# Router logits of an attention and mixture-of-experts kernel: per tile with the tokens stationary, or per batch of four tiles with the experts stationary

## The chip, the core and the metric

The kernel runs on one core of a Trainium2 chip. A time is the device time of one execution in microseconds. The profile is one execution recorded by the hardware profiler: PE is TensorE's matmuls, PEld its weight loads, DVE VectorE, ACT ScalarE, POOL GpSimd, SP the SyncE queue. "L689" is line 689 of the kernel file.

## The reference

Chunked attention over 8 batches, 8 heads, 576 positions and 64 dimensions (chunks of 64), then a router over 8 experts and the chosen expert's two-layer network for each of the 4608 tokens. All data is float32.

```
scores = q_c @ k_c^T / sqrt(64)              # per chunk of 64
attn   = softmax(scores);  out = attn @ v_c
x      = out as (4608 tokens, 512)
xn, en = x / |x|,  expert_emb / |expert_emb|
logits = xn @ en^T / tau                     # (4608, 8)
expert = argmax(logits)
gate   = softmax(logits)[expert]
y      = gate * (relu(x @ w1[expert]) @ w2[expert])    # 512 -> 1024 -> 512
```

## The kernel before

**Tiles and stages.** The 4608 tokens are 36 tiles (NT) of 128 tokens. A first stage runs attention and routing for tile after tile and writes each token's row, with its eight logits, to a place in DRAM (`spots`) that belongs to its expert. A second stage reads groups of 64 rows of one expert each, two experts at a time, and multiplies them by w1 and w2. The second stage isn't edited.

**The order of the first stage** is written out by hand (a manual schedule: each engine runs its instructions in program order). The loop at L1011 goes over t from -3 to NT + 2 and works on several tiles at once. In iteration t PE does, in this order: `turn_a(t)` (four transposes of the attention weights, L634), `turn_qk(t + 3)` (four transposes of k and four of q, L592), `logits(t - 2)` (L689), `scores(t + 2)` (32 records, L608), every fourth time `place` (L725 to L740), `turn_x(t - 1)` (four transposes of the attention output, L677) and `values(t)` (L648). A float32 matmul leaves two records in the trace, a transpose one.

**Who evicts.** ACT copies aT (L636), kxT (L595) and xT (L679) out of PSUM, squares the row (L682) and takes the exponential (L628). DVE copies qxT (L597), takes the maximum of the scores and subtracts it (L616, L618), divides the output (L656 to L659, tile `xr`), and copies the logits of four tiles (L702). The transposes share three PSUM buffers (`tr`); scores and values have one each (`sc`, `pv`).

**The router.** A batch is four tiles (RB = 4), so there are nine. `logits(t)` multiplies the 128 tokens of a tile, xT (stationary, 128 columns), by the normalised experts enT (moving, 8 columns), in four steps over the 512 dimensions. The result lies tokens by experts in `rt_ps`, one PSUM bank. After the fourth tile `copy_logits` moves 128x32 values to SBUF, `pick` (five DVE instructions, L712 to L716) finds the chosen expert as `eqb`, and in the next iteration `place` turns that into places: PE counts ranks (L725 to L740), DVE makes addresses of them (L750 to L759). `put` writes one tile's rows per iteration with an indirect DMA from POOL (L788). The ring `xr` holds eight tiles.

**Loads.** q and k are loaded by POOL four tiles ahead (L569), v and later the weights and rows by SP (L581, L128, L153).

**The end of the stage.** In the last iterations parts of the first expert product stand between the attention steps (`early_parts`, `hidden_part`, L253). After the last `place`, DVE works out the groups (`groups`, `places`, L840 to L959).

Of the kernel before, what the change touches and what calls it, by code (L numbers as in the profile page):

```python
# [9 lines left out]
FP32 = mybir.dt.float32  # L10
# [8 lines left out]
P = 128  # L19
# [6 lines left out]
def kernel(  # L26
# [11 lines left out]
    nc = tc.nc  # L38
    B, H, S, Dh = q.shape
    E, D = moe_expert_emb.shape  # L40
# [3 lines left out]
    KD = D // P  # L44
    KF = F // P
    NT = N // P
    NCB = S // CH
    G = P // 2
    Q = 32
# [74 lines left out]
    def load_first(buf, rows):  # L124

        for s in range(2):
            e = (0, E - 1)[s]
            nc.sync.dma_start(out=whole(buf[s]), in_=rows[:, e : e + 1, :], max_dma_last_dim=4096)  # L128
# [313 lines left out]
    RB = 4  # L442
    sizes = [RB] * (NT // RB)
    batch_of = [(b, i) for b, n in enumerate(sizes) for i in range(n)]
    VW = 2 * Dh
    with (
# [14 lines left out]
        pad(qk_p, 40, "pad_qk")  # L461
        ident = one.tile([P, P], FP32, name="ident")
        make_identity(nc, ident)
        rt_ps = ps_l.tile([P, 4, RB, E], FP32, name="rt_ps")
        emb = one.tile([E, D], FP32, name="emb")
        emb_sq = one.tile([E, 1], FP32, name="emb_sq")
        emb_n = one.tile([E, 1], FP32, name="emb_n")
        tau_sb = one.tile([E, 1], FP32, name="tau_sb")
        enT = one.tile([P, KD, E], FP32, name="enT")


        onesb = one.tile([P, P], BF16, name="onesb")
# [83 lines left out]
        qk_t, qkT, v_t, st = {}, {}, {}, {}  # L556
# [30 lines left out]
        def turn_qk(t):  # L587
            for nm in ("kx", "qx"):
                a = qk_t.pop((nm, t))
                ps = ps_t.tile([P, NPAIR, P], FP32, tag="tr", name="tr")  # L590
                for i in range(NPAIR):
                    nc.tensor.transpose(ps[:, i], a[:, i * P : i * P + P], ident)  # L592
                x = wk.tile([P, NPAIR, P], FP32, tag=nm + "T", name=nm + "T")
                if nm == "kx":
                    nc.scalar.copy(x, ps)  # L595
                else:
                    nc.vector.tensor_copy(x, ps)  # L597
                qkT[nm, t] = x

        def scores(t):  # L600
            qx, kx = qkT.pop(("qx", t)), qkT.pop(("kx", t))
            ps = ps_s.tile([P, 2, 512], FP32, tag="sc", name="sc")
            sc = ps[:, :, 0 : NPAIR * CH].rearrange("p r (i k) -> p r i k", k=CH)
            for i in range(NPAIR):
                for par in range(2):
                    for c in range(2):
                        r0, c0 = CH * par, CH * c
                        nc.tensor.matmul(  # L608
                            sc[CH * c : CH * c + CH, par, i],
                            lhsT=qx[r0 : r0 + CH, i, c0 : c0 + CH],  # L610
                            rhs=kx[r0 : r0 + CH, i, c0 : c0 + CH],
                            start=True,
                            stop=True,
                        )
            mx = wk.tile([P, 2, NPAIR], FP32, tag="mx", name="mx")
            nc.vector.tensor_reduce(mx, sc, axis=AX.X, op=ALU.max)  # L616
            a = wk.tile([P, NPAIR, 2, CH], FP32, tag="a", name="a", bufs=3)
            nc.vector.tensor_tensor(  # L618
                a.rearrange("p i r k -> p r i k"),
                sc,  # L620
                mx.unsqueeze(3).to_broadcast([P, 2, NPAIR, CH]),
                ALU.subtract,
            )
            st[t] = {"a": a}
# [5 lines left out]
        def turn_a(t):  # L630
            d = st[t]
            ps = ps_t.tile([P, NPAIR, P], FP32, tag="tr", name="tr")
            for i in range(NPAIR):
                nc.tensor.transpose(ps[:, i], d["a"][:, i].rearrange("p r k -> p (r k)"), ident)  # L634
            aT = wk.tile([P, NPAIR, P], FP32, tag="aT", name="aT")
            nc.scalar.copy(aT, ps)  # L636
            d["aT"] = aT
# [35 lines left out]
        def turn_x(t):  # L673
            d = st[t]
            ps = ps_t.tile([P, KD, P], FP32, tag="tr", name="tr")
            for c in range(KD):
                nc.tensor.transpose(ps[:, c], d["x"][:, c * P : c * P + P], ident)  # L677
            xT = wk.tile([P, KD, P], FP32, tag="xT", name="xT")
            nc.scalar.copy(xT, ps)  # L679
            d["xT"] = xT  # L680
            junk = one.tile([P, D], FP32, tag="junk", name="junk")
            nc.scalar.activation(  # L682
                junk, d["x"], AF.Square, accum_out=xr[:, t % NX, D + SQ : D + SQ + 1]
            )

        def logits(t):
            d = st.pop(t)
            for c in range(KD):
                nc.tensor.matmul(  # L689
                    rt_ps[:, batch_of[t][0] % 2, batch_of[t][1]],  # L690
                    lhsT=d["xT"][:, c],
                    rhs=enT[:, c],
                    start=(c == 0),
                    stop=(c == KD - 1),
                )

        copied = {}

        def copy_logits(b):
            n, t = sizes[b], sum(sizes[:b])  # L700
            copied[b] = xr[:, t % NX : t % NX + n, D : D + E]
            nc.vector.tensor_copy(copied[b], rt_ps[:, b % 2, 0:n])  # L702

        def pick(b):

# [63 lines left out]
        def count_early():  # L769

            cnt = rt_ps[:, 3, 0]
            nc.tensor.matmul(cnt, lhsT=onesb, rhs=before, start=True, stop=True)

            nc.vector.tensor_scalar(full, cnt, -1.0, lim, ALU.mult, ALU.add)
            nc.vector.tensor_scalar(full, full, 0.0, float(P), ALU.max, ALU.min)
            with nc.allow_low_precision("whole numbers up to 36 + 128"):
                nc.vector.tensor_tensor(eqb_all[:, 0], full, ends_e, ALU.mult)
                nc.vector.tensor_tensor(before, before, eqb_all[:, 0], ALU.add)
# [192 lines left out]
        def turn_experts():  # L971
            ps = ps_t.tile([P, KD, P], FP32, tag="tr", name="tr")
            for c in range(KD):
                nc.tensor.transpose(ps[:, c, 0:E], emb[:, c * P : c * P + P], ident[0:E, 0:E])
            nc.vector.tensor_copy(enT, ps[:, :, 0:E])

        nc.scalar.dma_start(out=emb, in_=moe_expert_emb)
        nc.scalar.dma_start(out=tau_sb, in_=moe_tau.unsqueeze(0).to_broadcast([E, 1]))
# [21 lines left out]
        def early_parts(t, i):  # L1000

            for j, s, b in early_at.get((t, i), ()):
                if j not in early_ps:
                    pool, tag = ((ps_s, "sc"), (ps_v, "pv"))[j]
                    early_ps[j] = pool.tile([P, 2, 512], FP32, tag=tag, name="h2_ps")
                ps = early_ps[j][:, s].rearrange("p (b f) -> p b f", b=G // Q)
                hidden_part(j, s, b, w1_sb, None, None, ps)

        early_t = 26
        ends = {sum(sizes[: b + 1]) - 1: b for b in range(len(sizes))}  # L1010
        for t in range(-3, NT + 3):  # L1011

            if 0 <= t < NT:
                turn_a(t)
            if t == early_t - 1:
                count_early()
            if t + 3 < NT:
                turn_qk(t + 3)
                if t + 7 < NT:
                    load_qk(t + 7)  # L1020
            if 0 <= t - 2 < NT:
                logits(t - 2)
            if t - 2 in ends:
                copy_logits(ends[t - 2])
            if t == NT:
                turn_x(t - 1)
            early_parts(t, 0)
            if 0 <= t + 2 < NT:
                scores(t + 2)
            if t - 3 in ends:  # L1030
                place(ends[t - 3])
            if 0 <= t - 1 < NT - 1:
                turn_x(t - 1)
            if 0 <= t < NT:
                values(t)
                b = (2 * t + 2) // NCB + 1
                if b not in v_t and b < B and t > 1:
                    load_v(b)
            if t == NT - 8:
                load_first(w1_sb, w1_rows)  # L1040
            if t == NT - 6:
                load_first([w[0] for w in w2_sb], w2_rows)
            if 0 <= t + 2 < NT:
                weights(t + 2)
            if t - 2 in ends:
                pick(ends[t - 2])
            if early_t <= t < early_t + XBUF:
                load_early(t - early_t)

            put(1 if t < NT - 2 else 2)  # L1050
            if t == NT - 3:
                turn_xb(0)
                load_early(XBUF)
            if t == NT - 1:
                turn_xb(1)
            early_parts(t, 1)
            if t == -2:
                turn_experts()
            if t == 0:
                constants()  # L1060
            if t == 1:
                clear_first()
# [26 lines left out]
    with (  # L1089
# [18 lines left out]
        for j in range(LEAST - 1):  # L1108
            n = j + 2
# [104 lines left out]
```

## Time and profile before

| what | value |
|---|---|
| median of 3 runs | 685.06 us (678.24 to 685.06) |
| profiled execution | 682.05 us, span 680.2 us |
| mean granted TensorE clock | 0.98 |
| PE busy | 643.7 us (95%) |
| PEld busy | 365.1 us (54%) |
| DVE busy | 423.5 us (62%) |
| ACT busy | 441.9 us (65%) |
| POOL busy | 155.7 us (23%) |
| logits, L689, PEld | 288 records, 35.8 us busy, 196 ns mean |
| logits, L689, PE | 288 records, 35.5 us busy, 250 ns mean |

How to read it: the rows of tenths on the page cut the span into 40 slices of 17 us, and a digit is the busy share of a slice. In a timeline, a line is start (us), length (us), engine, line, instruction, output<-inputs, shapes and number of records; a bracket at its end is the time for which the engine stood idle before it, and what released it. Records of pipelined matmuls overlap, so the cost of a step is read from one start to the next.

### The profile page before, as it was taken

To read this page: it belongs to the slowest core of one execution; us is meant where nothing else is said; L and a number is where in the kernel's file an instruction comes from. 1 tells how busy PE (TensorE), PEld (TensorE's weight loads), DVE (VectorE), ACT (ScalarE), POOL (GpSimd) and SP (SyncE) were. 2 spreads that over 40 slices of the span, in tenths; PEclk is the share of its full clock that TensorE was granted. 3 is DMA by queue.
4 is the path that set the end of the run, shared out by engine and by line. 5 is a ranking of instruction groups with operands and counts; after the bars stand their busy time and mean duration, and the time that the engine had idled before them with its cause. 6 is when DMAs were issued, how large, how long until landed. Compare 5 with 4: busy or idle time off the path is not lost. (4 is left out here: it accounts for less than half of the span.)

```text
span 680.2 us, 24833 instructions
## 1 busy us (share of the span) xinstructions
PE 643.7 (95%) x9735; PEld 365.1 (54%) x9735; DVE 423.5 (62%) x1139; ACT 441.9 (65%) x767; POOL 155.7 (23%) x237
## 2 busy tenths in 40 slices
PE   5889999999998989999999999989999999999993
PEld 5779999988543434544544444344444443444441
DVE  4648888878389654566676556777565567565430
ACT  5536666665223675767787776878877767867740
POOL 7727777742241000100000010000100000100101
PEclk9869999999999999999999999999999999999997
DMA  9977998989826821111778111775831114411101
GB/s 262 254 181 216 267 266 267 262 235 338 334 100 236 324 66 43 52 43 41 279 277 299 50 49 41 269 287 175 325 122 45 50 46 160 172 41 35 49 29 37
DMA packets 94590, 112.66 MB, mean 166 GB/s; under 512 B 52364, under 2 KB 72588, under 8 KB 94456
## 3 DMA queue, kind: packets, MB, share of 16 engines
q1 hardware_dynamic: 82728, 72.84, 33.7%
q0 software_dynamic: 11696, 38.04, 16.9%
q8 instruction: 81, 1.33, 0.8%
q14 instruction: 53, 0.43, 0.2%
q10 hardware_dynamic: 32, 0.02, 0.0%
HBM read 334.71 MB, written 22.69 MB: 525 GB/s over the span
## 5 line engine op out<-in xcount | busy, mean ns | idle before, releaser
L413 PE MATMUL y_ps<-w,hT 128*32 128x512 f32 (+1 forms) x2368 | 274.4, 587 | 2.2 <-DMA w<-in_moe_w_dram 2.2
L361 ACT ACTIVATE h<-C 64x256 f32<-64x256 f32 x264 | 178.7, 677 | 93.2 <-DVE C L374 68.1
L413 PEld LDWEIGHTS y_ps<-w,hT 128*32 128x32 f32 x2368 | 87.5, 110 | 159.5 <-issue 145.7
L428 POOL DMA_INDIRECT out_dram<-y,spot x36 | 34.9, 968 | 436.0 <-ACT y L421 203.3
L374 DVE TENSOR_TENSOR C<-C,h 128x256 f32<-128x256 f32 x231 | 96.1, 417 | 46.7 <-DVEq L299 39.7
L342 PE MATMUL h<-w,S 128*32 128x256 f32 x1056 | 101.1, 381 | 2.0 <-DVE w L291 2.0
L342 PE MATMUL h<-sums,xbT 128*32 128x256 f32 x1056 | 101.1, 383 | 0.0
L342 PE MATMUL h<-w,xbT 128*32 128x256 f32 x1056 | 80.6, 380 | 6.3 <-ACTq L299 5.1
L368 DVE STREAM_TRANSPOSE hT<-h 128x512 f32<-128x512 f32 x66 | 46.7, 708 | 45.5 <-ACT h L361 45.4
L342 PEld LDWEIGHTS h<-w,xbT 128*32 128x32 f32 x1056 | 40.3, 110 | 43.0 <-ACTq L299 12.7
L342 PEld LDWEIGHTS h<-w,S 128*32 128x32 f32 x1056 | 48.0, 110 | 25.3 <-DVE w L291 1.5
L342 PEld LDWEIGHTS h<-sums,xbT 128*32 128x32 f32 x1056 | 48.5, 111 | 22.5 <-issue 0.8
L679 ACT COPY xT<-tr 128x512 f32<-128x512 f32 x36 | 21.1, 586 | 53.8 <-PE tr L677 53.8
L227 DVE TENSOR_SCALAR rn<-rn 128x1 f32<-128x1 f32 x37 | 5.7, 153 | 72.8 <-ACT rn L224 72.8
L342 PE MATMUL h<-sums,S 128*32 128x256 f32 x528 | 49.9, 379 | 0.0
L788 POOL DMA_INDIRECT spots<-xr,dest x36 | 37.1, 1030 | 37.9 <-ACT aT L636 14.9
L203 DVE STREAM_TRANSPOSE xbT<-xin 128x256 f32<-128x256 f32 x73 | 44.2, 644 | 0.5 <-DVE hT L368 0.5
L224 ACT ACT_TABLE_LOAD x34 | 43.6, 1283 | 1.0 <-issue 0.4
L231 ACT ACT_TABLE_LOAD x34 | 43.6, 1283 | 0.6
L421 ACT ACTIVATE y<-y_ps,gate 128x512 f32<-128x512 f32 (+1 forms) x37 | 25.2, 682 | 28.8 <-issue 12.7
L689 PEld LDWEIGHTS rt_ps<-enT,xT 128*128 128x128 f32 x288 | 35.8, 196 | 1.1 <-issue 0.8
L569 POOL DMA_DIRECT2D kx<-in_k_dram x36 | 31.4, 874 | 20.4 <-PE tr L592 20.3
(198 smaller groups left out, 843.4 us busy)
## 6 DMA issues: line engine op xcount, KB each, us to landing
w<-in_moe_w_dram SPq DMA_DIRECT2D x74, 2048.0 KB
next_w<-in_moe_w_dram SPq DMA_DIRECT2D x67, 2048.0 KB
xin<-spots SPq DMA_DIRECT2D x158, 64.0 KB
qx<-in_q_dram POOLq DMA_DIRECT2D x32, 256.0 KB
v<-in_v_dram SPq DMA_DIRECT2D x56, 144.0 KB
kx<-in_k_dram POOLq DMA_DIRECT2D x28, 256.0 KB
spot<-spots SPq DMA_DIRECT2D x80, 4.0 KB
spots<-blank SPq DMA_DIRECT2D x2, 576.0 KB
```

Of the source, the lines that this page charges most:

```text
L203: nc.vector.transpose(xT[:, :, cols].rearrange("p c (b i) -> p b c i", i=Q), t[:, s * (D // 2) : (s + 1) * (D // 2)].rearrange("p (b i c) ...
L224: nc.scalar.activation(rn, spot[:, j % SPOTS, SQ : SQ + 1], AF.Sqrt)
L231: nc.scalar.activation(sh, sh, AF.Exp, accum_out=gate)
L342: nc.tensor.matmul(ps[t0 : t0 + Q], lhsT=a[:, c, s], rhs=w[:, r], start=c == 0, stop=c == KD // 2 - 1,)
L361: nc.scalar.activation(h[b][G * v : G * v + G, s].rearrange("p (k i) -> p k i", i=Q), x[G * s : G * s + G].rearrange("p (i k) -> p k i", i=Q),
L368: nc.vector.transpose(hT.rearrange("p k (s b i) -> p b s k i", b=2, i=Q)[:, b], h[b].rearrange("p s (k i) -> p s k i", i=Q),)
L374: nc.vector.tensor_tensor(out, a, b, op)
L413: nc.tensor.matmul(ps[Q * r : Q * r + Q, 0:w], lhsT=d["hT"][:, c, Q * t0 : Q * t0 + Q], rhs=w2_sb[s][buf_of(j)][:, c, d0 : d0 + w], start= ...
L428: ins = nc.gpsimd.indirect_dma_start(out=to, out_offset=bass.IndirectOffsetOnAxis(ap=at, axis=0), in_=y[:, 0:w], in_offset=None, bounds_ch ...
L569: eng.dma_start(out=x[done : done + n], in_=src[b, :, s : s + n, :].rearrange("h p d -> p h d"),)
L689: nc.tensor.matmul(rt_ps[:, batch_of[t][0] % 2, batch_of[t][1]], lhsT=d["xT"][:, c], rhs=enT[:, c], start=(c == 0), stop=(c == KD - 1),)
L788: ins = nc.gpsimd.indirect_dma_start(out=spots, out_offset=bass.IndirectOffsetOnAxis(ap=at, axis=0), in_=m, in_offset=None, bounds_check=S ...
```

## The change

The logits of a batch are computed together, once every four iterations. The stationary operand is now enT, padded with zeros from 8 to 32 columns; the moving operand is a tile's xT with its 128 tokens. Each of the four tiles of the batch has its own quarter of the array's columns, so that its logits land on its own 32 PSUM partitions (`lq_ps`, experts by tokens). ACT copies these 128x128 values to SBUF (`lq`). After `scores`, PE transposes them back into `lt_ps` (tokens by tile and expert), and DVE copies the eight experts of each tile out. `logits` and `copy_logits` run only in iterations whose t - 2 ends a batch; `copy_logits` moves from ahead of the early parts and scores to behind them. xT gets five buffers in place of two. All of `rt_ps`, `lq_ps` and `lt_ps` lie in one PSUM bank.

```
-        rt_ps = ps_l.tile([P, 4, RB, E], FP32, name="rt_ps")
+        rl_ps = ps_l.tile([P, 4 * RB * E + 2 * P], FP32, name="rt_ps")
+        rt_ps = rl_ps[:, 0 : 4 * RB * E].rearrange("p (a n e) -> p a n e", a=4, n=RB)
+        lq_ps, lt_ps = (rl_ps[:, o : o + P] for o in (4 * RB * E, 4 * RB * E + P))
...
-        enT = one.tile([P, KD, E], FP32, name="enT")
+        enT = one.tile([P, KD, Q], FP32, name="enT")
...
-            xT = wk.tile([P, KD, P], FP32, tag="xT", name="xT")
+            xT = wk.tile([P, KD, P], FP32, tag="xT", name="xT", bufs=RB + 1)
...
-        def logits(t):
-            d = st.pop(t)
+        def logits(b):
+            t = sum(sizes[:b])
+            xT = [st.pop(t + i)["xT"] for i in range(RB)]
             for c in range(KD):
-                nc.tensor.matmul(
-                    rt_ps[:, batch_of[t][0] % 2, batch_of[t][1]],
-                    lhsT=d["xT"][:, c],
-                    rhs=enT[:, c],
-                    start=(c == 0),
-                    stop=(c == KD - 1),
-                )
+                for i in range(RB):
+                    nc.tensor.matmul(
+                        lq_ps[Q * i : Q * i + Q],
+                        lhsT=enT[:, c],
+                        rhs=xT[i][:, c],
+                        start=(c == 0),
+                        stop=(c == KD - 1),
+                    )
+            lq = wk.tile([P, P], FP32, tag="lq", name="lq", bufs=1)
+            nc.scalar.copy(lq, lq_ps)
+            copied[b] = lq
...
         def copy_logits(b):
             n, t = sizes[b], sum(sizes[:b])
+            nc.tensor.transpose(lt_ps, copied[b], ident)
             copied[b] = xr[:, t % NX : t % NX + n, D : D + E]
-            nc.vector.tensor_copy(copied[b], rt_ps[:, b % 2, 0:n])
+            nc.vector.tensor_copy(
+                copied[b], lt_ps.rearrange("p (n e) -> p n e", e=Q)[:, 0:n, 0:E]
+            )
...
-            nc.vector.tensor_copy(enT, ps[:, :, 0:E])
+            nc.vector.memset(enT, 0.0)
+            nc.vector.tensor_copy(enT[:, :, 0:E], ps[:, :, 0:E])
...
-            if 0 <= t - 2 < NT:
-                logits(t - 2)
             if t - 2 in ends:
-                copy_logits(ends[t - 2])
+                logits(ends[t - 2])
             if t == NT:
                 turn_x(t - 1)
             early_parts(t, 0)
             if 0 <= t + 2 < NT:
                 scores(t + 2)
+            if t - 2 in ends:
+                copy_logits(ends[t - 2])
             if t - 3 in ends:
                 place(ends[t - 3])
```

## The prediction, made before the changed kernel ran

> **What bounds the kernel now.** I began with the page: the rows of busy tenths, to see which stage the change is in.
>
> ```profile
> PE   5889999999998989999999999989999999999993
> DVE  4648888878389654566676556777565567565430
> PEclk9869999999999999999999999999999999999997
> DMA  9977998989826821111778111775831114411101
> ```
>
> Forty slices of 17 us. Attention and routing fill the first eleven; after that PE works through the experts at 9 tenths, and nothing there is edited. Up to slice ten DVE stands at 8 and DMA at 8 or 9 beside a PE at 9: three engines near their limit, so shortening PE's work need not shorten the stage. The busy time by stretches gives the busy us of PE, PEld, DVE, ACT and POOL (instructions in brackets), then the granted clock, the DMA share and GB/s:
>
> ```profile
> 100.00:120.00 20.00, 20.00 (x440) 18.40 (x432) 17.08 (x44) 13.19 (x30) 12.87 (x19) 1.00 0.91 261
> ```
>
> Next the timeline of PE over one tile, read from start to start (the durations overlap):
>
> ```profile
> 106.19 0.60 PE L592 MATMUL tr<-ident,kx 128*128 128x128 f32 x4
> 106.63 0.60 PE L592 MATMUL tr<-ident,qx 128*128 128x128 f32 x4
> 107.07 0.96 PE L689 MATMUL rt_ps<-enT,xT 128*128 128x8 f32 x8
> 107.95 0.69 PE L608 MATMUL sc<-kxT,qxT 64*64 64x64 f32 x32
> 108.58 0.66 PE L677 MATMUL tr<-ident,xr 128*128 128x128 f32 x4
> ```
>
> No line has idle time before it. A tile is sc 0.63, x 0.58, pv 0.63, a 0.49, kx 0.44, qx 0.44, logits 0.88: 4.09 us; four tiles and one placing (0.14) make a batch of 16.5 us. DVE's timeline shows who follows:
>
> ```profile
> 107.27 0.69 DVE L597 COPY qxT<-tr 128x512 f32<-128x512 f32 x1
> 108.72 0.69 DVE L616 TENSOR_REDUCE mx<-sc 128x8 f32<-128x512 f32 x1 [0.76 <-PE sc L608]
> ```
>
> PE sets the pace, but DVE's slack is only that 0.76 us in a plain tile, and none in a tile with picking or placing.
>
> **Removed: four logits of one tile each.** The stationary operand is xT with 128 columns; eight experts stream through. Eight records in 0.88 us are 0.11 us each: weight loading. Without them qx would meet sc directly, and the first tiles show this:
>
> ```profile
> 17.58 0.60 PE L592 MATMUL tr<-ident,qx 128*128 128x128 f32 x4
> 18.11 0.69 PE L608 MATMUL sc<-kxT,qxT 64*64 64x64 f32 x32
> ```
>
> That is 0.53 us against 0.44 + 0.88, so a removal frees 0.79 us, four of them 3.17 us per batch.
>
> **Added: 32 records of 128 moving columns in four column quarters.** No row shows this form. The nearest is the expert product, four quarters, 256 columns:
>
> ```profile
> 213.27 1.05 PE L342 MATMUL h<-w,S 128*32 128x256 f32 x16
> 214.13 1.05 PE L342 MATMUL h<-sums,xbT 128*32 128x256 f32 x16
> ```
>
> 16 records in 0.86 us are 54 ns each; with 512 columns (y_ps) 64 records take 6.83 us, 107 ns. Columns set the price, so 128 would cost 27 ns. The score matmuls, with only 64 columns, still need about 17 to 20 ns, so a floor starts to show. I take 30 ns: 0.96 us. The ends are 27 ns (0.86 us) and 54 ns, no gain from halving the columns (1.73 us).
>
> **A rule against it**: "Mode switching requires drain" (Trainium skill, TensorEngine Tiling (Array Packing), Tiling Modes, Key Properties). The batch adds one switch, since qx, logits and sc now use three tilings. The row: qx to sc is 0.53 where kx to qx is 0.44, so a switch costs 0.09 us; 32 expert records after a transpose took 1.86 us, not 1.73, so 0.13. I take 0.2 for both switches, of which 0.09 was there. The page gives no figure; if the drain were a whole record (379 ns in the expert rows) the two would be 0.76, and a batch 0.56 us dearer. The rows decide, the rule stays in the range.
>
> **Added: eviction, turn and copy.** ACT copies 128x128: its 128x256 copies take 369 ns, so I take 0.25, between 0 and 0.37. It waits for the logits; behind it stand the xT copy, square and exp of the tile, with 1.40 us of idle before them now. PE does scores (0.63) before the turn, longer than the copy with its hand-over (0.32), so nothing waits; were that cover gone, it would cost PE 0.3 us per batch. The turn is one transpose of the four in 0.44: 0.12 with hand-over. The DVE copy stays 0.19 but moves behind mx and sub. No DMA is added, and no issue on SP or POOL passes another. The longer xT ring has no cost of its own. The 128x128 memset at the start is 0.1 to 0.2 us of DVE, hidden by the wait shown below.
>
> **A batch, summed.** PE alone: 16.5 - 3.17 + 0.96 + 0.11 + 0.12 = 14.5 us. DVE alone, start to start: 3.09 a tile, plus 0.16 copy, 0.99 pick, 0.86 placing: 14.4 us. Equal totals do not run in step. Following both queues through four tiles, PE meets two new waits. (1) From scores of the batch tile to placing, PE needs 0.63 + 0.12 + 0.58 + 0.63 + 0.49 + 0.44 + 0.53 + 0.63 = 4.05; DVE, released 0.78 after that start, needs mx 0.79, sub 0.61, copy 0.16, rs 0.43, xr 0.61, pick 1.07 and a hand-over of 0.03: 4.48. Wait 0.43. (2) turn_x of the next tile needs its xr: from the pick, DVE does qxT 0.65, mx 0.79, sub 0.61, placing 0.86, rs 0.43, xr with hand-over 0.81, together 4.15. PE gets there after 0.11 (hand-over to placing) + 0.14 + 0.58 + 0.63 + 0.49 + 0.44 + 0.53 + 0.63 = 3.55. Wait 0.59. So 14.5 + 0.43 + 0.59 = 15.55: 0.95 us gained per batch, not 1.95.
>
> **Which batches count.** The first does not:
>
> ```profile
> 39.05 0.48 PE L648 MATMUL pv<-v,aT 64*64 64x65 f32 x4 [2.06 <-DMA v<-in_v_dram]
> ```
>
> PE waits here for v whatever it saved before, so three of the four removals are lost. Then it runs at half clock to 48 us, and the batched logits fall into that: (0.96 + 0.11 + 0.12) x 2 = 2.4 us come in, the one removal left takes 0.79 x 2 = 1.6 out. With hand-overs 0.9 us is lost. Batches two to eight gain 7 x 0.95 = 6.65. The last:
>
> ```profile
> 166.46 0.18 PE L725 MATMUL rt_ps<-eqb_all,sltb 128*128 128x32 bf16 x1 [0.91 <-DVE eqb_all L716]
> 184.39 0.18 PE L725 MATMUL rt_ps<-eqb_all,sltb 128*128 128x32 bf16 x1 [0.76 <-DVE eqb_all L716]
> ```
>
> At 166 the freed logits only lengthen the wait, and the moved copy adds 0.16. The next two tiles free 0.65 and 0.85. At 184 the turn now stands behind the early expert parts: switch and transpose, hand-over, copy and pick make 1.7 us to placing instead of 0.9: 0.8 lost. Sum 0.5 gained. In all 6.65 + 0.5 - 0.9 = 6.25 us. Everything later follows PE and keeps its length. The profiled execution took 682.05 us (span 680.2): 675.8. Its median of runs is 685.06, 3.0 above it; the same distance gives **678.8 us**.
>
> **Rivals.**
> - **PE alone decides** (chance 0.2). If DVE's queue runs ahead more than I think, 7 x 1.95 + 0.5 - 0.9 = 13.2 us: 671.8. For: score banks are free 1.8 us before PE needs them (sub ends 106.11, next sc 107.95). Against: pick and placing are in one chain with PE.
> - **DMA becomes the bound** (0.15). A batch moves 4.3 MB (q, k, v 1.05 each, rows written 1.18): 264 GB/s at a share of 0.94. If that is all there is, 4.3 MB need 16.4 us, and 7 x 0.1 - 0.4 = 0.3 us is left: 684.8. Against: stretches of 4 us reach 305 to 323 GB/s, and loads are issued four tiles ahead.
> - **The clock halves once per batch: slower** (0.12). After the 0.91 us wait above came this:
>
> ```profile
> 168.00:170.00 2.00, 2.00 (x24) 1.02 (x20) 1.52 (x5) 0.46 (x2) 0.12 (x1) 0.50 0.76 225
> 170.00:172.00 2.00, 2.00 (x23) 0.97 (x15) 0.00 (x0) 0.03 (x1) 1.55 (x2) 0.67 0.93 300
> ```
>
> 1.0 + 0.66 us lost. The new waits, 0.43 and 0.59 within four us, could do the same in each of seven batches: 11.6 - 6.25 = 5.4 slower, 690.4; it decides from 0.9 us lost per batch. The skill (TensorE: Matmul & The Clock Gate, Part 1) ties the drop to an idle window of about 3.4 us: by that, nothing. By the row, 0.91 us sufficed once; but waits of 0.76 and 0.78 at 184 and 187 left the clock at 1.00. The same page (Part 4) says that transposes do not count as busy, and transposes are what remains; yet from 8 to 20 us, without logits, the clock stood at 1.00.
> - **The quarters do not run side by side** (0.05): 32 x 107 ns = 3.4 us, a batch 0.5 us longer, about 689. Against: the expert rows above.
>
> **Numbers.** The forecast has 0.48, the rivals 0.2, 0.15, 0.12 and 0.05. About 1% is what a measurement of this kernel tells from no change. The forecast is 0.9% below; its own ends (records of 54 ns, drains) leave nearly nothing, others reach 2%. I give 0.17 of its chance to faster and 0.31 to the same; the first rival is faster, the DMA case the same, the last two slower. Range 671 to 689.
>
> **What would show it.** Right: logits as 32 records in 0.9 to 1.1 us, four times fewer groups; per batch about 15.5 us between placings; new idle before the placing (on eqb_all) and before turn_x (on xr); DVE near 0.93 busy; no wait of the turn for ACT. Wrong: records over 45 ns; a clock under 1.00 between 60 and 140 us; PE waiting for q, k or v after 50 us; or experts after 200 us of another length.

## The result, and the profile after

| what | before | after |
|---|---|---|
| median of 20 runs each, us | 683.32 (678.24 to 688.48) | 676.97 (672.64 to 681.12) |
| profiled execution (span), us | 682.05 (680.2) | 673.1 (671.3) |
| PE busy from 60 to 140 us | 79.96 of 80 | 75.11 of 80 |
| DVE busy from 60 to 140 us | 67.73 | 68.67 |

The ratio of after to before is **0.9912, 95% interval 0.9886 to 0.9939**. The forecast, 678.8 against 685.06, was a ratio of 0.9909. The two profiled executions lie further apart (8.9 us) than the medians (6.35 us), because the one of after was 3.9 us below its median and the one of before only 1.3. So the medians give the size of the gain, and the profiles its places.

From the page of the changed kernel, the rows of tenths that answer to those of before:

```profile
PE   6869998998898989999999999999999999999993
DVE  4738888986598536547675566757655666565430
PEclk9969999999999989999999999999999999999997
DMA  9978999989818711113786111777811115411111
```

PE has more 8s in the first stage where it had 9s, and DVE is about as it was. The busy time by stretches (us of PE, PEld, DVE, ACT and POOL, then granted clock, DMA share, GB/s):

```profile
100.00:120.00 20.00, 18.23 (x444) 15.47 (x441) 16.61 (x41) 13.72 (x32) 14.98 (x21) 1.00 0.93 266
120.00:140.00 20.00, 19.20 (x477) 16.21 (x481) 17.38 (x45) 14.01 (x33) 15.55 (x22) 1.00 1.03 287
```

PE was 20.00 of 20.00 before. Now it idles for 1.2 us in twenty over 60 to 140 us, the clock is full, and the DMA share is 1.03 in the second row without any wait of PE for q, k or v after 50 us. In the first row 1.19 us of PE's idle time is a single gap at 107.88 us, within the scores, for which the trace names no releaser.

PE's timeline from a batch's logits on (start, length, operation, records; a bracket is the idle time before it):

```profile
137.03 0.60 PE L595 MATMUL tr<-ident,qx 128*128 128x128 f32 x4
137.56 1.08 PE L695 MATMUL rt_ps<-xT,enT 128*32 128x128 f32 x32
138.57 0.69 PE L611 MATMUL sc<-kxT,qxT 64*64 64x64 f32 x32
139.19 0.33 PE L710 MATMUL rt_ps<-ident,lq 128*128 128x128 f32 x1
139.36 0.60 PE L680 MATMUL tr<-ident,xr 128*128 128x128 f32 x4
...
142.99 0.18 PE L737 MATMUL rt_ps<-eqb_all,sltb 128*128 128x32 bf16 x1 [0.33 <-DVE eqb_all L728]
```

From start to start, the 32 records of four tiles' logits take 1.01 us (L695) and the transpose back takes 0.17 (L710). No bracket stands before the transpose, though it needs ACT's copy of the logits. The group of that copy, from 50 to 140 us (count, busy us and mean ns, then ACT's idle time before it):

```profile
L703 ACT COPY lq<-rt_ps 128x128 f32<-128x128 f32 x6 | 1.6, 265 | 2.9 <-PE rt_ps L695 2.9
```

265 ns of copying lie beside 0.63 us of scores. What PE does wait for in the stage, by the list of PE's waits from 52 to 150 us (us in total, times, longest):

```profile
PE rt_ps L737 <- DVE eqb_all L728: 1.9, 6, 0.4
PE tr L680 <- ACT kxT L598: 1.4, 3, 0.6
PE tr L680 <- DVE xr L662: 1.2, 3, 0.6
PE sc L611 <- issue: 1.2, 1, 1.2
```

Both foretold waits are there: on `eqb_all` ahead of the placing, 0.32 us on average over six, and ahead of `turn_x`, 0.43 on average over six (a seventh, of 0.27, has no named releaser). The second is not always released by `xr`: three times of six ACT's kxT copy, which frees the `tr` buffer, came last.

**Where the difference lies.** The nine placings mark the batches in both timelines:

| stretch | before | after | gained | foretold |
|---|---|---|---|---|
| start to first placing | 50.83 | 49.34 | 1.49 | -0.9 |
| first to eighth placing | 115.63 | 108.26 | 7.37 | 6.65 |
| eighth to ninth | 17.93 | 16.84 | 1.09 | 0.5 |
| ninth placing to the end of the span | 495.8 | 496.9 | -1.05 | 0 |
| sum | 680.2 | 671.3 | 8.9 | 6.25 |

### The profile page after: what moved, and what is told of

The parts are those of the page before. It is cut to its first block, busy times and chain, and to the rows that moved or that the text cites. A ratio compares the mean times of both kernels' runs of the same rounds, so it can differ in the third digit from the quotient of the medians.

```text
span 671.3 us, 24844 instructions
## 1 busy us (share of the span) xinstructions
PE 623.0 (93%) x9744; PEld 346.2 (52%) x9744; DVE 421.3 (63%) x1140; ACT 443.8 (66%) x776; POOL 155.3 (23%) x237
## 5 line engine op out<-in xcount | busy, mean ns | idle before, releaser
L413 PEld LDWEIGHTS y_ps<-w,hT 128*32 128x32 f32 x2368 | 93.2, 110 | 153.6 <-issue 123.8
L342 PE MATMUL h<-w,S 128*32 128x256 f32 x1056 | 98.1, 379 | 1.8 <-DVE w L291 1.8
L342 PE MATMUL h<-sums,xbT 128*32 128x256 f32 x1056 | 97.0, 379 | 0.0
L224 ACT ACT_TABLE_LOAD x34 | 43.6, 1283 | 0.9 <-issue 0.4
L231 ACT ACT_TABLE_LOAD x34 | 43.6, 1283 | 0.6
L651 PE MATMUL pv<-v,aT 64*64 64x65 f32 x1152 | 28.1, 226 | 9.0 <-DMA v<-in_v_dram 7.4
```

The costliest lines, as they stand in the source:

```text
L224: nc.scalar.activation(rn, spot[:, j % SPOTS, SQ : SQ + 1], AF.Sqrt)
L231: nc.scalar.activation(sh, sh, AF.Exp, accum_out=gate)
L342: nc.tensor.matmul(ps[t0 : t0 + Q], lhsT=a[:, c, s], rhs=w[:, r], start=c == 0, stop=c == KD // 2 - 1,)
L413: nc.tensor.matmul(ps[Q * r : Q * r + Q, 0:w], lhsT=d["hT"][:, c, Q * t0 : Q * t0 + Q], rhs=w2_sb[s][buf_of(j)][:, c, d0 : d0 + w], start= ...
L651: nc.tensor.matmul(pv[CH * c : CH * c + CH, par, i], lhsT=d["aT"][r0 : r0 + CH, i, CH * c : CH * c + CH], rhs=v_t[b][r0 : r0 + CH, i, cb, ...
```

## The experiments

Three groups ran on three chips, with the kernel before beside each: its medians were 684.62, 694.25 and 690.15 us. Ratios are to the kernel before of the same group; the changed kernel itself was not timed in these groups beyond one run in the third, so its 0.9912 comes from other runs. A period is the time from one placing to the next, read from one profile; it is called undisturbed where it holds no gap of 0.3 us or more without a releaser and q and k are still loaded.

### Is it the form, the batching, or both?

**The old form, batched.** In the kernel before, the four tiles' logits are put together; each keeps its tokens stationary and eight moving columns.

```diff
-            xT = wk.tile([P, KD, P], FP32, tag="xT", name="xT")
+            xT = wk.tile([P, KD, P], FP32, tag="xT", name="xT", bufs=RB + 1)
...
-            if 0 <= t - 2 < NT:
-                logits(t - 2)
             if t - 2 in ends:
+                for i in range(RB):
+                    logits(t - 2 - RB + 1 + i)
                 copy_logits(ends[t - 2])
```

> The kernel before, but the logits of four tiles run together once per batch, still with the tokens stationary (32 records of 128 loaded columns, some 0.1 us each). PE's work per batch is the same 16.5 us. Theory (DVE falls behind after a long PE tile): the uneven order alone costs PE about 1.0 us per batch of new waits, before placing (on eqb_all) and before turn_x, so 17.5 us between placings and 5 to 8 us more in all (ratio 1.010). Rival (PE's sum alone decides): 16.5 us between placings, ratio 1.000.

Measured: 712.51 us, ratio 1.0456 (1.0377 to 1.0534). The first period is 17.61 us, near what the theory gave, and its waits are 0.40 on `eqb_all` and 0.33 on `xr`: batching alone brings the new waits and no gain. Most later periods are 18.65 to 20.52 us. PE's timeline shows why:

```profile
82.16 3.64 PE L689 MATMUL rt_ps<-enT,xT 128*128 128x8 f32 x32
85.72 0.69 PE L608 MATMUL sc<-kxT,qxT 64*64 64x64 f32 x32
86.35 0.66 PE L677 MATMUL tr<-ident,xr 128*128 128x128 f32 x4
86.94 1.15 PE L648 MATMUL pv<-v,aT 64*64 64x65 f32 x32
88.01 1.11 PE L634 MATMUL tr<-ident,a 128*128 128x128 f32 x4
```

pv takes 1.07 us to the next start and tr a 0.91, where the kernel before has 0.63 and 0.49. The stretches of the same kernel (columns as above):

```profile
84.00:86.00 2.00, 2.00 (x33) 1.98 (x36) 0.17 (x1) 0.00 (x0) 1.82 (x4) 1.00 0.72 228
86.00:88.00 2.00, 2.00 (x66) 1.66 (x56) 1.41 (x3) 0.96 (x2) 0.39 (x1) 0.74 0.87 309
88.00:90.00 2.00, 2.00 (x14) 1.99 (x11) 1.64 (x7) 1.35 (x4) 0.00 (x0) 0.50 0.53 125
```

Half clock sets in 2.9 to 4.9 us after such a run of eight-column matmuls starts, that is, around its end, in seven of the eight batches up to 190 us; it lasts 3.4 us, twice 6.8. From 60 to 150 us, 8.5 us are lost so. The expectation had not foreseen this: it had a ratio of 1.010. It is the rival "the clock halves once per batch", in a kernel in which PE had no idle time in the row before it. The Trainium skill (TensorE: Matmul & The Clock Gate, Part 1) ties the drop to a window of idle time; here the row of PE reads 2.00 of 2.00. Whether the clock takes the few columns, or another property of that run, for idle time was not tried.

**The new form, not batched.** The changed kernel with each tile's logits in its own iteration, alone in its quarter of the columns; eviction and transpose back stay once per batch.

```diff
-        def logits(b):
-            t = sum(sizes[:b])
-            xT = [st.pop(t + i)["xT"] for i in range(RB)]
+        def logits(t):
+            b, i = batch_of[t]
+            xT = {i: st.pop(t)["xT"]}
...
+            if i < RB - 1:
+                return
             lq = wk.tile([P, P], FP32, tag="lq", name="lq", bufs=1)
...
-            if t - 2 in ends:
-                logits(ends[t - 2])
+            if 0 <= t - 2 < NT:
+                logits(t - 2)
```

> The changed kernel, but each tile's logits run in its own iteration with the experts stationary, in the tile's quarter alone; copy, turn and pick stay once per batch. Theory (the saving is that four quarters run side by side): 8 records alone in a quarter cost about 107 ns each, 0.86 us, no less than before, and every tile pays a switch more, so about 17 us between placings, ratio 1.005. Rival (the saving is that 32 instead of 128 columns are loaded): 0.2 to 0.3 us per tile and about 14.6 us between placings, ratio 0.98.

Measured: 688.65 us, ratio 1.0067 (1.0032 to 1.0102), slower than before; undisturbed periods of 17.38 us. The timeline of PE:

```profile
63.17 1.06 PE L694 MATMUL rt_ps<-xT,enT 128*32 128x128 f32 x8
64.16 0.69 PE L611 MATMUL sc<-kxT,qxT 64*64 64x64 f32 x32
```

One tile's eight records take 0.99 us, as long as the 32 records of four tiles (1.01). Alone in its quarter a record costs 0.12 us, like the old form's 0.11; side by side four cost that together. So the gain is neither the form nor the batching but four quarters at work at once: the kernel is slower with either half alone, though in the old form half clock adds to that.

### Is the transpose back hidden?

The transpose moves from behind the scores to directly behind the logits.

```diff
             if t - 2 in ends:
                 logits(ends[t - 2])
+                copy_logits(ends[t - 2])
...
-            if t - 2 in ends:
-                copy_logits(ends[t - 2])
```

> The changed kernel, but the turn and the DVE copy stand right behind the logits, ahead of the scores. Theory: PE now waits for ACT's copy, which the scores covered: about 0.4 to 0.5 us per batch of new idle on lq, and DVE's copy comes ahead of mx; between placings about 15.9 us in place of 15.5, 3 us more than the changed kernel, ratio to before 0.995. Rival (PE has slack there because DVE sets the pace): no longer than the changed kernel, 15.5 us.

Measured: 677.53 us, ratio 0.9913 (0.9875 to 0.9951); the first three periods are 15.77 to 16.07. PE's waits from 52 to 150 us:

```profile
PE rt_ps L710 <- ACT lq L703: 2.4, 6, 0.4
```

Without scores as cover the hand-over to ACT is paid, 0.4 us in every batch; the first three periods are 15.88 on average where after's undisturbed ones are 15.38 (15.13 to 15.61). The four later ones hold other gaps too and are 15.74 to 17.15. In the time of the whole kernel this isn't resolved: 9 x 0.4 = 3.6 us is half a per cent, and the interval is wider than that.

### What holds the batch at 15.4 us: the chain through DVE

**ACT copies qxT in the placing iteration**, 0.65 us less for DVE between pick and the next `xr`.

```diff
-                if nm == "kx":
+                if nm == "kx" or t - 6 in ends:
                     nc.scalar.copy(x, ps)
```

> The changed kernel, but in the iteration with the placing ACT copies qxT in place of DVE (one tile in four). Theory (PE's two new waits come from DVE): the wait before turn_x, 0.3 to 0.6 us, goes; about 14.9 us between placings, 4 us less in all than the changed kernel, ratio to before 0.985. Rival (DMA is the bound at 15.5 us): PE or POOL waits for q, k or v instead, 15.5 us. Rival (ACT is as full as DVE): a wait on kxT or aT takes its place, 15.5 us or more.

Measured: 673.49 us, ratio 0.9868 (0.9808 to 0.9928); three undisturbed periods, 14.80 to 15.05. PE's waits from 52 to 150 us:

```profile
PE rt_ps L738 <- DVE eqb_all L729: 1.6, 5, 0.4
PE pv L652 <- issue: 1.4, 2, 1.1
PE tr L681 <- issue: 0.6, 1, 0.6
```

The wait of `turn_x` is gone, both on `xr` and on kxT, and the one ahead of the placing stays. The mean of the three periods, 14.89, is 0.5 us below after's 15.38 and within 0.4 of the 14.5 worked out for PE alone. With the disturbed periods, from the first to the eighth placing, 106.50 us stand against after's 108.26, 0.25 a batch. In the time of the whole kernel the difference is not resolved: the interval holds after's 0.9912.

**The same copy, two iterations later**: as much work taken from DVE, but outside the chain.

```diff
-                if nm == "kx":
+                if nm == "kx" or t - 8 in ends:
                     nc.scalar.copy(x, ps)
```

> The changed kernel, but ACT copies qxT in a plain iteration (two after the placing) in place of the one with the placing. Theory (the wait before turn_x comes from one chain: pick, qxT, maximum, placing, xr): the copy is not in that chain, the wait stays, about 15.5 us between placings, ratio 0.991. Rival (DVE's total load per batch is the bound): the same relief as in the other place, 14.8 to 14.9 us, ratio 0.987.

Measured: 686.9 us, ratio 0.9936 (0.9902 to 0.9971). The first six periods are 16.37 to 17.67 us, not the 15.5 expected; on this chip the unedited changed kernel has such periods as well (see below). PE waits 0.26 to 0.60 us ahead of `turn_x` in each batch, as in after; from 52 to 150 us:

```profile
PE tr L681 <- issue: 1.5, 4, 0.5
PE tr L681 <- ACT kxT L599: 1.0, 2, 0.6
PE tr L681 <- DVE xr L663: 0.5, 1, 0.5
```

One of the four without a named releaser belongs to another tile. On the same chip, the kernel with both edits below has the copy in the chain; there the same list has

```profile
PE tr L681 <- issue: 0.3, 1, 0.3
PE tr L681 <- ACT kxT L599: 0.2, 1, 0.2
```

and only the second of these stands ahead of that `turn_x`. So it is the place in the chain, not DVE's total, that sets this wait.

**One more DVE instruction ahead of pick**, in the kernel before (dve_before) and in the changed one (dve_after): a maximum over 128x512 whose result nobody reads, 0.68 us.

```diff
+        idle = one.tile([P, 1], FP32, name="idle")
...
         def pick(b):
...
+            nc.vector.tensor_reduce(idle, blank[:, 0:D], axis=AX.X, op=ALU.max)
```

> The kernel before with one more DVE instruction per batch (a 128x512 maximum ahead of pick, about 0.66 us, result unused). Theory: DVE has over 1.5 us of slack per batch, but pick comes later and placing waits a little: 16.5 to 16.8 us between placings, 0 to 2 us in all. Rival (PE alone decides): 16.5 us.

> The changed kernel with the same DVE instruction. Theory (DVE's chain sets the two waits): all 0.66 us shows, about 16.2 us between placings in place of 15.5, 4 to 5 us more in all than the changed kernel, ratio to before 0.998. Rival (PE alone decides, or DMA): 15.5 us, unchanged.

Measured: 694.55 us, ratio 1.0035 (0.9989 to 1.0081), on before; 692.25 us, ratio 0.9981 (0.9943 to 1.0019), on after. Against 0.9912 without it, after pays 0.0069 of 694 us, 4.8 us, or 0.53 of 0.68 us in each of nine batches; before pays 0.27, with an interval that includes nothing. The 0.9912 was measured in other runs than these, and the two costs are not told apart by their intervals. The first six periods, 16.67 to 18.93 us on before and 16.82 to 17.99 on after, are all but one longer than expected (16.5 to 16.8, and 16.2) and do not separate the kernels either. So this experiment does not show that the changed kernel has less slack on DVE; that rests on the two copies of qxT.

### The first batch: is the saving swallowed by the wait for v?

`clear_first` issues its DMAs on SP's queue in the same stretch as the first loads of v. It is moved two iterations later, in the kernel before (v_first_before) and in the changed one (v_first_after).

```diff
-            if t == 1:
+            if t == 3:
                 clear_first()
```

> The kernel before, but SP clears the first places two iterations later, so that the second batch of v is issued some 4 us earlier and does not share the DMA engines with 1.3 MB of writes. The wait for v at 37 to 39 us should go or shrink by 2 us, and with it the half clock to 48 us: 2 to 6 us less.

> The changed kernel with the same move. Theory (the first batch's saving is swallowed by the wait for v, 7 us in the changed kernel): 2 to 3 us more is gained here than in the kernel before by the same move, so the first placing comes about 3 us ahead of that one's. Rival (v comes when DMA can bring it, whatever the order): v still lands near 38 us and nothing is gained in either.

Measured: 682.3 us, ratio 0.9839 (0.9762 to 0.9916), and 677.39 us, ratio 0.9775 (0.9702 to 0.9849). The first placing of the one and of the other, in PE's timelines:

```profile
45.25 0.18 PE L725 MATMUL rt_ps<-eqb_all,sltb 128*128 128x32 bf16 x1
```

```profile
40.27 0.18 PE L737 MATMUL rt_ps<-eqb_all,sltb 128*128 128x32 bf16 x1 [0.22 <-DVE eqb_all L728]
```

That is 5.0 us apart, where after and before are 1.49 apart. 1.7 of the 5.0 is half clock in v_first_before alone (0.57 from 36 to 40 us); 3.3 remains, near the 3 expected. PE's own sum gives 3.17 - 0.96 - 0.11 - 0.12 = 2.0 of it; the rest is not traced to a cause. In v_first_before PE still waits for v, as long as in before (2.06) but 2.8 us earlier:

```profile
36.25 0.33 PE L648 MATMUL pv<-v,aT 64*64 64x65 f32 x2 [2.21 <-DMA v<-in_v_dram]
```

In v_first_after no wait for v is left, and the saving of the first batch shows. In the whole time this is not resolved: 0.9775 to 0.9839 is a ratio of 0.9935, no other than that of the change by itself. What the edit shows beside it: moving `clear_first`'s DMA issues is worth about as much as the change, or more (12 us of the medians). The first placing of v_first_before comes 5.6 us ahead of that in before's profile, on another chip; where the rest of the 12 us lies is not known.

**Both edits**, the later `clear_first` and ACT's copy of qxT, on the changed kernel (diffs as above).

> The changed kernel with both edits that helped: ACT copies qxT in the iteration with the placing, and SP clears the first places two iterations later. The two act at different places (each batch, and the first wait for v), so they should add: ratio to before about 0.968 to 0.975. If a common bound (DMA) lies just behind, no better than the earlier clearing alone, 0.978.

Measured: 679.43 us, ratio 0.9821 (0.9772 to 0.9871). The first placing is at 38.89 us, but the sum of the two gains is not there. The profile has four stretches of half clock between 74 and 174 us, which lose 8.5 us, and a gap of 2.7 us ahead of pv without a releaser; and it ran on the chip on which the changed kernel gains little per batch (next section). It beats before, but is not shown to beat v_first_after or the qxT edit alone.

### Both kernels profiled again

In the second and third group most periods were longer than in the first profiles, so both kernels were profiled again, unchanged, in the third.

> The kernel before once more, one profile. If the half clock at 168 to 171 us belongs to the kernel's order, it is there again; if it is a matter of where the clock's window falls, it is absent or elsewhere. Between placings again 16.5 us.

> The changed kernel once more, one profile. Between placings again 15.1 to 15.6 us, apart from single stalls. If the absence of a half clock after 155 us belongs to the change, it is absent again; if not, one of 1 to 2 us lost turns up near the waits of 1.8 and 1.4 us.

Measured: 689.63 us and 685.13 us, one run each. The first six periods are 16.47 to 17.27 us for before and 16.46 to 17.47 for after, where 15.1 to 15.6 was expected. From the first to the eighth placing before takes 119.37 us and after 119.69: the gain per batch is gone there. The 4.5 us between the two spans are 3.29 ahead of the first placing, 0.34 in the last batch and 1.19 behind it. After's wait on `eqb_all` is 1.2 to 1.6 us in five of six batches. DVE's waits from 52 to 150 us, of before and of after:

```profile
DVE rs L656 <- PE tr L592: 3.7, 4, 1.1
```

```profile
DVE rs L659 <- PE tr L595: 5.2, 5, 1.2
```

These waits were absent in the first profile of after, and that of before has one on rs, 0.8 us, for pv. In DVE's timeline of the changed kernel:

```profile
78.61 0.18 DVE L712 COPY xr<-rt_ps 128x32 f32<-128x32 f32 x1
80.01 0.17 DVE L659 TENSOR_SCALAR rs<-pv 128x8 f32<-128x8 f32 x1 [1.22 <-PE tr L595]
```

rs needs only pv, whose records end at 78.5 by the trace, yet it starts at 80.01; ACT's aT copy is released at 80.07 as well. It looks as if PE's results came out some 1.2 us late, about once per batch, between the copy of the logits and the pick. The wait falls into the chain of `rs`, `xr`, pick and placing, in which the changed kernel has no slack: over the first six periods it takes 1.3 us more per batch than in its first profile, before 0.1. What holds the results back is not settled; ends of matmuls are modelled in the trace, and the transpose that it names as the releaser writes nothing that rs needs.

## Why the prediction was right, and where it was not

**In the first profiles the mechanism was as described, and the total was met.** The steps by their numbers:

- **32 records at 30 ns, 0.96 us.** 1.01 us, or 32 ns a record: the price still falls with the columns down to 128, a little less than in proportion (54 ns at 256, so 27). The rival that the quarters do not run side by side would have had 3.4 us; the kernel with one quarter at a time shows what that is (0.99 us a tile).
- **The switches, 0.2 us.** From qx to the logits 0.53 us, 0.09 above a plain transpose's 0.44: a switch costs what the rows of before said, and the logits' 1.01 hold the other. A drain of a whole record (379 ns) at each switch does not fit these rows.
- **Copy 0.25 on ACT, hidden; transpose 0.12.** 265 ns, 0.17, no wait; uncovered it is 0.4 per batch, foretold as 0.3.
- **Waits of 0.43 and 0.59.** 0.32 and 0.43 on average: the DVE chain was right, and for the second wait shown by the edit that shortens it, but the waits were put 0.11 and 0.16 us too long. Of these 0.27 the logits and the transpose took back 0.10, and single gaps without a releaser (1.19 us in after, 0.82 in before) 0.05, so that a batch gained 1.05 us and not 0.95. The second wait was put on `xr` alone; half the time ACT's kxT copy is last, so its price rests on two engines that come at the same time.
- **PE alone, 14.5 us a batch.** Not what the change does, but where it stands with one qxT copy moved (14.89). The first rival, PE alone, had this floor right; that DVE runs far enough ahead to reach it was wrong.
- **DMA and clock.** DMA's share rose from 0.94 to 1.00 over 60 to 140 us with 281 GB/s, and it stayed no bound. The clock was 1.00 there: half clock didn't come from waits of 0.3 to 0.6 us. The old form batched shows that it can come once per batch, and dve_after has it beside two placings, from 68.3 and from 102.4 us, with waits of 1.83 and 2.04 us; a wait of 1.64 in the second profile of after left the clock at 1.00. One argument against the rival was misread: from 8 to 20 us the clock row says 1.00, but up to 11 us the groups ran at half speed:

```profile
8.06 1.06 PE L592 MATMUL tr<-ident,kx 128*128 128x128 f32 x4
8.91 1.06 PE L592 MATMUL tr<-ident,qx 128*128 128x128 f32 x4
```

  That is 0.85 us from start to start, as at 41 us at a clock of 0.50, and not 0.44. Only from 11.3 us on do transposes and scores alone run at full speed.

**Three terms failed, in different directions.**

*The first batch, -0.9 where 1.49 was gained.* That v swallows the saving held: from PE's timeline of after,

```profile
38.29 0.93 PE L651 MATMUL pv<-v,aT 64*64 64x65 f32 x8 [5.58 <-DMA v<-in_v_dram]
```

The wait has grown from 2.06 to 5.58 us and pv is done at 40.37, against 40.10. The failed step was "then it runs at half clock to 48 us". In before that is so: half clock lasts from 38.2 to 48.4 us. In after it lasts as long, 10.2 us, but from 34.4 to 44.6. PE's long wait for v begins four us earlier there, and so does half clock; more of it falls into the wait. The batched logits still run in it (1.73 us), most of what follows does not. The stretch from 44 to 48 us of before, and of after:

```profile
44.00:48.00 4.00, 4.00 (x72) 3.40 (x73) 1.87 (x5) 1.43 (x4) 0.29 (x2) 0.50 0.73 191
```

```profile
44.00:48.00 4.00, 4.00 (x100) 3.42 (x93) 2.22 (x6) 1.99 (x6) 0.56 (x2) 0.92 0.47 138
```

0.50 against 0.92 in four microseconds is 1.7 us of PE's work; without it after would stand 0.2 behind. Place and length of this stretch also differ between two profiles of one kernel: in the second ones it lasts 13.7 us in before (35.7 to 49.4) and 6.8 in after (36.7 to 43.6). It should have been a range, not a value.

*The last batch, 0.5 where 1.09 was gained, for another reason.* Before lost 1.66 us at half clock at 168 to 172 us; after's first profile has none. Without that, after is 0.57 slower there. The freed time of the last tiles was mis-sized, not the turn behind the early parts:

```profile
168.45 4.32 PE L253 MATMUL h_ps<-w,xbT 128*32 128x256 f32 x64
172.71 0.33 PE L710 MATMUL rt_ps<-ident,lq 128*128 128x128 f32 x1
174.44 0.18 PE L737 MATMUL rt_ps<-eqb_all,sltb 128*128 128x32 bf16 x1 [1.40 <-DVE eqb_all L728]
```

1.73 us from turn to placing is the 1.7 foretold. But the 0.65 and 0.85 that the two tiles before it free do not reach the placing: the early parts are longer (4.32 us for 64 records and once 2.33 for 32, where before has 3.66 and 1.93 at full clock), and `aT` and `h` are waited for, 0.24 and 0.17 us. Together 1.5 us, as much as the two tiles free. Why these parts run longer was not tested. The half clock at 168 us itself is no mark of the kernel before: both second profiles lose 1.7 us to it between 169 and 176 us, so of the 1.09 nothing can be put down to the change.

*"Everything later keeps its length".* From the ninth placing to the end after takes 1.05 us more. One wait in that part differs, 3.1 us of y_ps behind DVE's queue (L299) in after, 2.2 us behind the weights' DMA in before; it was not tested. In the second profiles after takes 1.19 us less there, so the 1.05 is no mark of the change.

In the profiles the misses are 2.4 + 0.6 - 1.05 = 1.9 us at the ends and 0.7 in the batches, which with 6.25 makes 8.9. The medians have 6.35, near the 6.25 of the sum. That the sum is met this closely is luck in part: in the second profiles nothing is gained in the batches and most of the 4.5 us ahead of the first placing, and misses in the ends have cancelled.

## What to carry to other kernels

What a narrow matmul costs depends on how many quarters of the columns run at once: here 32 records of 128 columns in four quarters cost 1.01 us, and eight records in one quarter 0.99. With one piece alone the form gained nothing; two or three were not tried. When work is taken out of an engine that is 100% busy, follow the engine behind it through one period before counting the gain: of 1.95 us freed per batch 0.95 was foretold and 1.05 came, and one DVE copy moved out of the chain gave back 0.5 in undisturbed periods. A change that leaves the next engine no slack is exposed to what delays that engine: on another chip none of the 1.05 was left. Time freed ahead of a wait for a load is not gained until the load comes earlier; here moving a few DMA issues by two iterations gave a ratio of 0.9839, more than the saving that the wait had hidden.

## What the runs showed of the hardware beyond that

- Half clock came without idle time on PE: around the end of 3.64 us of 32 matmuls with eight moving columns each (in the batched old form, half clock from 87.0 to 90.4 us), in seven of eight batches of one profile. In the kernel before, the same 32 records stand apart in groups of eight, and the clock is at 1.00 from 60 to 150 us.
- Stretches of half clock came in lengths of about 3.4, 6.8, 10.2 and 13.7 us, multiples of 3.4, in all fourteen profiles (read in windows of 1 us, from 20 to 200 us). So such a stretch costs PE 1.7 us of work or a multiple of it. Its place differs between profiles of the same kernel: between 167 and 176 us one is there in three of the four profiles of before and after, and near 40 us it lasts 6.8 to 13.7 us.
- In the second and third group DVE's `rs` often waited about 1 us (up to 1.8) past the modelled end of pv, with a later transpose named as its releaser, in both kernels; in the third group in most batches. What releases it, the trace doesn't show; it stays open.
